# Keeping each 32-column block of a triangular inverse contiguous in SBUF

## The chip, the core and the metric

The kernel runs on one core of a Trainium2 chip. The metric is the device time of one execution in microseconds (us). The engines are TensorE (PE; its weight loads are shown as PEld), VectorE (DVE), ScalarE (ACT), GpSimd (POOL) and SyncE (SP, which issues the DMAs); each works through its own instructions in order. SBUF is the memory on the core with 128 partitions, PSUM the smaller one that TensorE writes.

## The reference, cut to what matters

Three stages follow each other: a linear recurrence over 768 steps for 32 heads of size 40, a channel mix, and an attention with four gated heads. The change touches the first alone:

```python
for t in range(S):                      # S = 768, state is (B, H, 40, 40)
    y[:, :, t] = np.einsum('bhd,bhde->bhe', rt, state)
    Sa = np.einsum('bhde,bhe->bhd', state, at)
    state = state * wt[:, :, None, :] - np.einsum('bhd,bhe->bhde', Sa, bt) \
            + np.einsum('bhd,bhe->bhde', vt, kt)
```

## The kernel before

The recurrence is done in 12 chunks of 64 steps. A chunk of half of the heads (16, as 8 pairs in the two halves of the partitions) is a unit `u`; there are 24 units, two to a chunk, and four units make a group `g`. Inside a chunk, the steps depend on each other through a unit lower triangular matrix of 64x64 per head, which has to be inverted. It is cut into two 32x32 diagonal blocks (inverted) and the 32x32 block below them (`m21`, used as it is).

- `front(u)` prepares a unit: scans for the decays on DVE (L152, L164), products (L172, L173), transposes on PE (L179, L189), and the matrices of the chunk as matmuls into PSUM (`pg`, L200). ACT evicts `pg`: the two diagonal blocks into `LX[g]` (L207, eight instructions a unit), the block `m21` (L210, four) and `ga` (L213).
- `lanes(g)` inverts all 128 x 2 diagonal blocks of a group at once on DVE. A 32x32 transpose (L226) brings `LX[g]` into `L`, so that each partition holds one block row by row. Thirty steps `s` follow, each a product (L231) and a sum (L233) over `(31 - s) x s` elements; memsets set the diagonal to 1 and what lies above it to 0 (L235, L239). A second transpose (L242) writes the inverses to `tf`.
- `core(u)` is the serial part. For each half `i` of 32 rows it multiplies by the inverse: 16 matmuls with 32x32 blocks of `tf` as weights (L276; each shows as two weight loads and two matmuls, so 32 of each a half). Between the halves come 16 matmuls with `m21` as weights (L270), which have the same sizes. ACT evicts `pw` at L256, L272, L279 and L283.
- `outs(u)` makes the outputs (L307 to L340).

`LX`, `L` and `tf` are 128 x 32 x 32 floats. In `L` a partition holds one block as `(t, s)`. In `LX` and in `tf` the two free axes are the column `t` within a block and the number `x` of the block in the group.

The strings `FIRST`, `STEADY` and `TAIL` say in which order the pieces of the sequences are written for a chunk; the instructions of PE keep that written order, those of the other engines are set by a scheduler at build time. After the recurrence, at about 480 us, the channel mix and the attention follow; they share no tile with the change.

Of the kernel before, what the change touches and what calls it, by code (L numbers as in the profile page):

```python
# [15 lines left out]
AF = mybir.ActivationFunctionType  # L16
# [12 lines left out]
PP = 8  # L29
WLEN = PP * C + 2 + PP  # L30
LDW = 3 * PP * C + WLEN
HP = PP // 2
# [13 lines left out]
def recurrence(ctx, tc, ld, vin, rv, ident, xs, keep, wpool, mix):  # L46

    nc = tc.nc
# [59 lines left out]
    BK, GA, PC, LX, M21, TF = {}, {}, {}, {}, {}, {}  # L108
# [33 lines left out]
    def front(u):  # L142

        g, uu = divmod(u, GU)
        c, bp = divmod(u, NBP)
        t = slot(u)
        f3 = t[:, :3 * PP * C].rearrange("p (k q t) -> p k q t", k=3, t=C)
        w = t[:, 3 * PP * C:3 * PP * C + PP * C + 2]
        last = t[:, 3 * PP * C + PP * C + 2:]

        P = keep.tile([128, PP, C], F32, tag="P", bufs=2, name=f"P{u}")
        nc.vector.tensor_tensor_scan(P.rearrange("p s t -> p (s t)"), w[:, :PP * C], onehot, 0.0, op0=OP.mult,  # L152
                                     op1=OP.add)
        pc = PC[u] = const.tile([128, PP, 2], F32, tag="pc", bufs=AHEAD + 3, name=f"pc{u}")
        nc.vector.tensor_scalar(pc[:, :, 0], P[:, :, C - 1], -1.0, None, op0=OP.mult)
        nc.vector.tensor_tensor(pc[:, :, 1], pc[:, :, 0], last, op=OP.mult)
        rc = fpool.tile([128, PP, 2], F32, tag="rc", bufs=2, name=f"rc{u}")
        nc.vector.reciprocal(rc, pc)
        E = etile
        early = u < GU  # L160
        ih = invhot.rearrange("p (s t) -> p s t", t=C)
        nc.vector.tensor_copy(ih[:, :, C - 2:], rc)
        er = E.rearrange("p s t -> p (s t)")[:, ::-1]
        nc.vector.tensor_tensor_scan(er, w[:, PP * C + 1:1:-1], invhot[:, ::-1], 0.0, op0=OP.mult, op1=OP.add)  # L164
        nc.vector.tensor_copy(E[:, :, C - 1], rc[:, :, 1])
        bkt = keep.tile([128, PP, 2, C], F32, tag="bkt", bufs=2, name=f"bkt{u}")
        if u >= GU:
            blank(u)
        ga = GA[u]
        for r in range(2):  # L170
            q = slice(64 * r, 64 * r + 64)
            nc.vector.tensor_tensor(ga[q, r], f3[q, 2], P[q], op=OP.mult)  # L172
        latest["dve"] = nc.vector.tensor_tensor(bkt.rearrange("p q k t -> p k q t"), f3[:, :2],  # L173
                                                E[:, None].to_broadcast([128, 2, PP, C]), op=OP.mult)
        yield

        pt = ps.tile([128, 4, 2, 64], F32, tag="f", bufs=3, name=f"pt{u}")
        for p in range(4):
            nc.tensor.transpose(pt[:, p].rearrange("p r e -> p (r e)"),  # L179
                                P[:, 2 * p:2 * p + 2].rearrange("p b t -> p (b t)"), ident)  # L180
        nc.scalar.activation(xs[bp][:, c].rearrange("p (a b d) -> p a b d", a=4, b=2), pt[:, :, :, :D], AF.Copy,
                             scale=-1.0)
        yield

        BK[u] = wpool.tile([128, PP, 2, D], F32, tag="bk", bufs=AHEAD + 4, name=f"bk{u}")
        for h in range(2):
            pb = ps.tile([128, HP, 128], F32, tag="f", bufs=3, name=f"pb{u}_{h}")
            for p in range(HP):
                nc.tensor.transpose(pb[:, p], bkt[:, h * HP + p].rearrange("p k t -> p (k t)"), ident)  # L189
            latest["act"] = nc.scalar.activation(BK[u][:, h * HP:h * HP + HP],  # L190
                                                 pb.rearrange("p q (r e) -> p q r e", r=2)[:, :, :, :D], AF.Copy)
            yield

        m21 = M21[u] = const.tile([128, PP, 32], F32, tag="m21", bufs=AHEAD + 1, name=f"m21{u}")
        if uu == 0:
            LX[g] = fpool.tile([128, 32, 32], F32, tag="lx", name=f"lx{g}")
        for h in range(2):
            pg = ps.tile([128, HP, 2, C], F32, tag="o" if early else "f", bufs=3, name=f"pg{u}_{h}")
            for p in range(HP):
                nc.tensor.matmul(pg[:, p], bkt[:, h * HP + p].rearrange("p k t -> p (k t)"),  # L200
                                 ga[:, :, h * HP + p], start=True, stop=True)
            hs = slice(h * HP, h * HP + HP)
            for r in range(2):
                for i in range(2):
                    q = slice(64 * r + 32 * i, 64 * r + 32 * i + 32)
                    x0 = uu * PP + h * HP
                    nc.scalar.activation(LX[g][q, :, x0:x0 + HP].rearrange("p t q -> p q t"),  # L207
                                         pg[q, :, r, 32 * i:32 * i + 32], AF.Copy)
                q = slice(64 * r, 64 * r + 32)
                nc.scalar.activation(m21[q, hs], pg[q, :, r, 32:], AF.Copy)  # L210
                z = slice(64 - 64 * r, 128 - 64 * r)
                if not early:
                    nc.scalar.activation(ga[z, r, hs], pg[z, :, r], AF.Copy)  # L213
                    if h:
                        latest["pool"] = nc.gpsimd.affine_select(ga[z, r], ga[z, r], [[0, PP], [1, C]], OP.is_gt, 0.0,  # L215
                                                                 base=0, channel_multiplier=-1)
                else:
                    nc.vector.tensor_tensor(ga[z, r, hs], pg[z, :, r],
                                            mask[z, None, :].to_broadcast([64, HP, C]), op=OP.mult)
            yield  # L220

    def lanes(g):

        L = fpool.tile([128, 32, 32], F32, tag="lt", name=f"lt{g}")
        Lf = L.rearrange("p t s -> p (t s)")
        nc.vector.transpose(Lf, LX[g].rearrange("p t x -> p (t x)"))  # L226
        for s in range(1, 31):
            tmp = fpool.tile([128, 16 * 16], F32, tag="tmp", bufs=1, name=f"tmp{g}_{s}")
            n = 31 - s
            tv = tmp[:, :n * s].rearrange("p (t c) -> p t c", c=s)  # L230
            latest["dve"] = nc.vector.tensor_tensor(tv, L[:, s + 1:, s:s + 1].to_broadcast([128, n, s]),  # L231
                                                    L[:, s:s + 1, :s].to_broadcast([128, n, s]), op=OP.mult)
            nc.vector.tensor_tensor(L[:, s + 1:, :s], L[:, s + 1:, :s], tv, op=OP.add)  # L233
            yield
        nc.vector.memset(Lf[:, ::33], 1.0)  # L235
        b = 16
        while b:

            nc.vector.memset(bass.AP(L.tensor, L.offset + b, [list(L.ap[0]), [66 * b, 16 // b], [32, b], [1, b]]), 0.0)  # L239
            b //= 2  # L240
        tf = TF[g] = tfs[g % 2]
        nc.vector.transpose(tf.rearrange("p t x -> p (t x)"), Lf)  # L242
        yield

    def core(u):

        g, uu = divmod(u, GU)
        c, bp = divmod(u, NBP)
        ga, bk, tf, U, T = GA[u], BK[u], TF[g], uv[u % 4], xu[bp]
        pw = ps.tile([128, PP, D], F32, tag=f"c{bp}", bufs=1, name=f"pw{u}")  # L250
# [4 lines left out]
        w0 = const.tile([128, PP, D], F32, tag="w0", bufs=2, name=f"w0{u}")  # L255
# [4 lines left out]
        for r in range(2):  # L260
            q = slice(64 * r, 64 * r + 64)
            nc.vector.tensor_copy(T[q, :, r, :D], U[q, :, r])

        for i in range(2):
            qs = [slice(64 * r + 32 * i, 64 * r + 32 * i + 32) for r in range(2)]
            if i:
                for p in range(PP):
                    for r in range(2):
                        q0 = slice(64 * r, 64 * r + 32)
                        nc.tensor.matmul(pw[qs[r], p], M21[u][q0, p], U[q0, p, r], start=False, stop=True,  # L270
                                         skip_group_check=True)
                nc.scalar.activation(w0, pw, AF.Copy)  # L272
                yield
            for p in range(PP):
                for r in range(2):
                    nc.tensor.matmul(pw[qs[r], p], tf[qs[r], :, uu * PP + p], w0[qs[r], p], start=p == 0,  # L276
                                     stop=True, skip_group_check=True)
            for r in range(2):
                nc.scalar.activation(U[qs[r], :, r], pw[qs[r]], AF.Copy)  # L279
            if i:  # L280
                for r in range(2):
                    q, z = slice(64 * r, 64 * r + 64), slice(64 - 64 * r, 128 - 64 * r)
                    nc.scalar.activation(T[z, :, r, :D], pw[q], AF.Copy)  # L283
            yield
        if c < NC - 1:
# [6 lines left out]
            for r in range(2):  # L292
                q = slice(64 * r, 64 * r + D)
# [646 lines left out]
```

## Time and profile before

| | us |
|---|---|
| median of 3 runs | 964.96 (963.48 to 965.97) |
| span of the profiled execution, from its first to its last instruction | 957.7 |
| median less that span | 7.3 |
| recurrence within the span, roughly | 0 to 480 |
| VectorE, TensorE, ScalarE busy over the span | 670.5, 810.1, 547.3 |

The time of the profiled execution itself is not listed; its span and the 7.3 us that lie around it stand for it. In the rows further down, "busy" is the time in which an engine works on instructions, "idle before" what it waited in front of them, with the instruction that ended the wait. The chain is the sequence of work that ended last, followed back from the end: time saved on it can shorten the execution, time saved beside it can not, until the chain moves. [...]

### The profile page before, as it was taken

What the parts mean: (1) busy time and instruction counts of PE and PEld (TensorE: products, weight loads), DVE (VectorE), ACT (ScalarE), POOL (GpSimd) and SP (SyncE); (2) the same over time, 40 slices, a digit from 0 to 9 for tenths busy, and PEclk for the clock granted to TensorE, in tenths of its full rate; (3) what the DMA queues carried; (4) which work ended last, traced back from release to release, by engine and by line L of the source; (5) the groups of instructions that cost most, each with busy time, mean ns of one, the idle gap of its engine ahead of it and who ended that gap; (6) DMA issues with size and microseconds to landing.
All of it is one profiled execution on the core that took longest, in us unless ns stands there. A gap on an engine that the chain in (4) does not pass through costs nothing.

```text
span 957.7 us, 22274 instructions
## 1 busy us (share of the span) xinstructions
PE 810.1 (85%) x8812; PEld 692.4 (72%) x8812; DVE 670.5 (70%) x1642; ACT 547.3 (57%) x1392; POOL 256.1 (27%) x332
## 2 busy tenths in 40 slices
PE   1554388884986889878899999999998999999997
PEld 1543377784886778857778788887887888788885
DVE  7988989789989976978766232322325886878874
ACT  2786187777677776646533242222315866767773
POOL 7001032123113210134434132201202633444330
PEclk9777579998898999979899999999999999999999
DMA  6423033423323221433321001000000001010001
GB/s 132 116 69 97 1 72 71 99 70 84 77 66 84 66 59 40 110 94 100 101 84 30 1 22 31 1 1 1 1 1 1 1 1 42 2 42 1 29 15 42
DMA packets 57895, 46.80 MB, mean 49 GB/s; under 512 B 45248, under 2 KB 48960, under 8 KB 55872
## 3 DMA queue, kind: packets, MB, share of 16 engines
q1 hardware_dynamic: 57792, 45.38, 18.8%
q8 instruction: 70, 1.15, 0.5%
q14 instruction: 33, 0.27, 0.1%
HBM read 41.44 MB, written 3.93 MB: 47 GB/s over the span
## 4 chain that ended last, share of the span: by engine, by line
PE 61%; DVE 16%; ACT 15%; DMA 5%; issue 3%; POOL 1%; SPq 0%; DVEq 0%; ACTq 0%; POOLq 0%
PE pn L322 5%; PE po L835 4%; PE pw L276 4%; ACT lx L207 3%; PE tp L822 3%; PE ph L635 3%; PE pa L654 3%; PE ph L632 3%; PE pa L653 3%; PE pa L652 3%; PE ph L633 3%; PE ph L631 3%; DMA ldt<-in_ld 3%; PE ps L782 2%; ACT ga L213 2%
## 5 line engine op out<-in xcount | busy, mean ns | idle before, releaser
L639 DVE SCALAR_TENSOR_TENSOR hl<-ph,hh 128x512 fp32r<-128x512 f32 x60 | 41.2, 690 | 122.4 <-ACT hh L638 121.1
L805 POOL TENSOR_TENSOR P<-P,sm 128x128 f32<-128x128 f32 (+2 forms) x92 | 82.9, 931 | 126.6 <-DVE sm L795 114.3
L215 POOL TENSOR_SCALAR_AFFINE_SELECT ga<-ga 64x512 f32<-64x512 f32 x40 | 36.6, 915 | 269.1 <-ACT ga L213 260.0
L276 PE MATMUL pw<-w,tf 32*32 32x40 f32 x1536 | 52.7, 235 | 53.5 <-DVE tf L242 45.3
L638 ACT ACTIVATE hh<-ph 128x512 fp32r<-128x512 f32 x60 | 35.2, 595 | 107.1 <-PE pa L654 95.9
L276 PEld LDWEIGHTS pw<-w,tf 32*32 32x32 f32 x1536 | 48.4, 150 | 58.6 <-issue 36.8
L207 ACT ACTIVATE lx<-pg 32x128 f32<-32x128 f32 x192 | 73.2, 381 | 14.9 <-PE pg L200 6.7
L786 ACT ACTIVATE P<-ps,mx 128x640 f32<-128x640 f32 (+4 forms) x96 | 60.5, 634 | 22.6 <-DVE mx L784 14.6
L189 PE MATMUL pb<-ident,bkt 128*128 128x128 f32 x192 | 33.8, 312 | 44.5 <-ACT ga L213 21.4
L279 ACT ACTIVATE uv<-pw 32x320 f32<-32x320 f32 x96 | 41.1, 428 | 52.7 <-PE pw L276 51.1
L233 DVE TENSOR_TENSOR lt<-lt,tmp 128x30 f32<-128x30 f32 (+9 forms) x180 | 63.5, 353 | 3.7
L784 DVE CUSTOM_DVE_ANT_0 ps<-ps,neg 128x640 f32<-128x640 f32 (+4 forms) x96 | 59.1, 640 | 7.5 <-PE ps L782 6.4
L231 DVE TENSOR_TENSOR tmp<-lt 128x30 f32<-128x30 f32 (+9 forms) x180 | 60.9, 338 | 3.2
L322 PE MATMUL pn<-rbd,uvt 128*128 128x128 f32 x384 | 60.8, 321 | 1.3 <-ACT uvt L311 1.3
L200 PE MATMUL pg<-ga,bkt 128*128 128x128 f32 x384 | 55.8, 304 | 5.7 <-ACT ga L213 5.5
L189 PEld LDWEIGHTS pb<-ident,bkt 128*128 128x128 f32 x192 | 23.4, 156 | 51.5 <-ACT ga L213 26.3
L322 PEld LDWEIGHTS pn<-rbd,uvt 128*128 128x128 f32 x384 | 57.1, 234 | 4.6 <-ACT uvt L311 2.2
L200 PEld LDWEIGHTS pg<-ga,bkt 128*128 128x128 f32 x384 | 52.7, 218 | 6.8 <-ACT ga L213 6.0
L822 PE MATMUL tp<-ident,P 128*128 128x128 f32 x336 | 52.0, 276 | 1.8 <-ACT pt L826 1.0
L668 POOL TENSOR_TENSOR t<-t,ul 128x512 f32<-128x512 f32 x12 | 15.3, 1295 | 119.9 <-DVE t L667 119.8
L654 PE MATMUL pa<-hh,w 128*128 128x512 f32 x120 | 47.0, 392 | 0.0
L632 PE MATMUL ph<-ul,w 128*128 128x512 f32 x120 | 46.8, 390 | 0.2 <-DVE ul L621 0.2
(220 smaller groups left out, 2364.2 us busy)
## 6 DMA issues: line engine op xcount, KB each, us to landing
ldt<-in_ld SPq DMA_DIRECT2D x44, 321.6 KB
uv<-in_vin SPq DMA_DIRECT2D x48, 80.0 KB
rbd<-in_rin SPq DMA_DIRECT2D x48, 80.0 KB
rpt<-in_rin SPq DMA_DIRECT2D x48, 80.0 KB
uvt<-in_rin SPq DMA_DIRECT2D x48, 80.0 KB
out<-o SPq DMA_DIRECT2D x24, 160.0 KB
ldt<-in_w SPq DMA_DIRECT2D x4, 512.0 KB
ldt<-in_w SPq DMA_DIRECT2D x5, 320.0 KB
```

The costliest lines, as they stand in the source:

```text
L200: nc.tensor.matmul(pg[:, p], bkt[:, h * HP + p].rearrange("p k t -> p (k t)"), ga[:, :, h * HP + p], start=True, stop=True)
L207: nc.scalar.activation(LX[g][q, :, x0:x0 + HP].rearrange("p t q -> p q t"), pg[q, :, r, 32 * i:32 * i + 32], AF.Copy)
L231: latest["dve"] = nc.vector.tensor_tensor(tv, L[:, s + 1:, s:s + 1].to_broadcast([128, n, s]), L[:, s:s + 1, :s].to_broadcast([128, n, s]) ...
L233: nc.vector.tensor_tensor(L[:, s + 1:, :s], L[:, s + 1:, :s], tv, op=OP.add)
L276: nc.tensor.matmul(pw[qs[r], p], tf[qs[r], :, uu * PP + p], w0[qs[r], p], start=p == 0, stop=True, skip_group_check=True)
L322: nc.tensor.matmul(pn[:, p], ut[:, h * HP + p].rearrange("p r t -> p (r t)"), rbd[u % 2][:, :, h * HP + p], start=True, stop=True)
L632: nc.tensor.matmul(ph, w[:, 0, f], ul[:, ft], start=False, stop=False)
L654: nc.tensor.matmul(pa[ft], w[:, 2 * DM - FT[2][0] + o:2 * DM - FT[2][0] + o + m], hh, start=False, stop=last)
L784: nc.vector.tensor_tensor_reduce(ps[:, :k], ps[:, :k], neg[:, S - k:], -1.0, 3e38, op0=OP.add, op1=OP.min, accum_out=mx[:, i:i + 1])
L786: nc.scalar.activation(P[blk][:, off[i] - off[i0]:off[i + 1] - off[i0]], ps[:, :k], AF.Exp, bias=mx[:, i:i + 1], scale=-1.0, accum_out=sm[ ...
L805: nc.gpsimd.tensor_tensor(p, p, sm[:, i:i + 1].to_broadcast([128, w]), op=OP.mult)
L822: nc.tensor.transpose(pt[:, j - j0], P[:, c:c + 128], ident)
```

## The change

`LX` and `tf` exchange their two free axes: from `(t, x)` to `(x, t)`, so that the 32 columns of a block lie next to each other. Four instructions see it.

- The ACT evictions into `LX` (L207) wrote single elements 32 floats (128 bytes) apart; they now write 128 elements in a row.
- The weight loads of `tf` (L276) read single elements 128 bytes apart; they now read 32 in a row.
- The first DVE transpose (L226) read in a row; it now reads single elements 128 bytes apart.
- The second DVE transpose (L242) wrote in a row; it now writes single elements 128 bytes apart.

```diff
-                    nc.scalar.activation(LX[g][q, :, x0:x0 + HP].rearrange("p t q -> p q t"),
-                                         pg[q, :, r, 32 * i:32 * i + 32], AF.Copy)
+                    nc.scalar.activation(LX[g][q, x0:x0 + HP], pg[q, :, r, 32 * i:32 * i + 32], AF.Copy)
...
-        nc.vector.transpose(Lf, LX[g].rearrange("p t x -> p (t x)"))
+        nc.vector.transpose(L, LX[g].rearrange("p x t -> p t x"))
...
-        nc.vector.transpose(tf.rearrange("p t x -> p (t x)"), Lf)
+        nc.vector.transpose(tf.rearrange("p x t -> p t x"), L)
...
-                    nc.tensor.matmul(pw[qs[r], p], tf[qs[r], :, uu * PP + p], w0[qs[r], p], start=p == 0,
+                    nc.tensor.matmul(pw[qs[r], p], tf[qs[r], uu * PP + p], w0[qs[r], p], start=p == 0,
```

No instruction is added, removed or moved: PE, DVE, ACT, POOL and SP each have the same instructions in the same order before and after. The changed program has one line less, so that what was L210 is L209 in it, and so on down; only L207 and the lines ahead of it keep their numbers.

On DVE, here is the end of `lanes` for the second group, with the transpose of the next group behind it. Before (the names are tiles with a number):

```order
L233 TENSOR_TENSOR lt_810<-lt_810,tmp_30_1150 128x30
L158 RECIPROCAL rc_1871<-pc_1868 128x16
L242 STREAM_TRANSPOSE tf_119<-lt_810 128x1024
L162 COPY invhot<-rc_1871 128x8x2
L172 TENSOR_TENSOR ga_1877<-ldt_84,P_1866 64x512 x2
L226 STREAM_TRANSPOSE lt_1650<-lx_1030 128x1024
```

The same place in the changed program:

```order
L232 TENSOR_TENSOR lt_810<-lt_810,tmp_30_1150 128x30
L158 RECIPROCAL rc_1871<-pc_1868 128x16
L241 STREAM_TRANSPOSE tf_119<-lt_810 128x32x32
L162 COPY invhot<-rc_1871 128x8x2
L172 TENSOR_TENSOR ga_1877<-ldt_84,P_1866 64x512 x2
L225 STREAM_TRANSPOSE lt_1650<-lx_1030 128x1024
```

Nothing moved. The transpose into `tf` now has an output pattern of 32 x 32 single elements; that of the other is on its input, which the row does not show.

## Rows read from the trace of the kernel before

**Rows 1.** Busy time of the engines in two stretches (instructions in brackets), granted clock.

```profile
112.00:340.00 228.00, 185.20 (x3545) 170.52 (x3546) 205.62 (x483) 172.47 (x483) 52.11 (x84) 0.89 0.32 73
363.00:416.00 53.00, 43.04 (x978) 38.85 (x974) 45.73 (x127) 33.64 (x89) 5.19 (x13) 0.91 0.30 77
```

**Rows 2.** Chain that ended last, shares by line in 0:112, 112:367 and 367:480 us.

```profile
by line: DMA ldt<-in_ld 23.1%; DVE P L152 11.0%; DVE ga L172 9.1%; DVE bkt L173 8.3%; DVE lt L233 7.7%; DVE tmp L231 6.9%; DVE E L164 6.3%; issue 4.6%; DVE pc L155 4.0%; DVE ga L218 3.3%; DVE invhot L162 2.0%; PE pb L189 1.7%; DVE rc L158 1
...
by line: ACT lx L207 12.8%; PE pn L322 12.4%; PE pw L276 9.2%; ACT ga L213 7.1%; PE pg L200 5.5%; ACT m L210 5.0%; issue 4.8%; ACT xu L283 4.7%; PE pb L189 4.6%; PE pw L270 4.4%; ACT uv L279 4.4%; ACT uvt L311 3.8%; PE pt L179 3.0%; ACT sbd
...
by line: PE pn L322 15.8%; PE pw L276 11.9%; DMA ldt<-in_w 11.0%; PE py L336 6.1%; PE py L332 4.3%; issue 4.1%; PE pv L307 3.8%; PE pw L270 3.5%; PE pw L253 3.0%; DVE ldt L455 3.0%; PE px L290 3.0%; DMA ldt<-in_v 2.7%; DMA room<-in_w 2.5%; 
```

**Rows 3.** Groups of instructions by line and shape: busy us, mean ns of one.

```profile
L207 ACT ACTIVATE lx<-pg 32x128 f32<-32x128 f32 x192 | 73.2, 381 | 14.9 <-PE pg L200 6.7 <-DVE ga L218 4.3 <-DVE lt L226 2.8
...
L213 ACT ACTIVATE ga<-pg 64x256 f32<-64x256 f32 x80 | 30.2, 378 | 1.0
...
L210 ACT ACTIVATE m<-pg 32x128 f32<-32x128 f32 x96 | 25.6, 267 | 1.2
...
L226 DVE STREAM_TRANSPOSE lt<-lx 128x1024 f32<-128x1024 f32 x6 | 7.4, 1241 | 4.7 <-ACT lx L207 4.3
L242 DVE STREAM_TRANSPOSE tf<-lt 128x1024 f32<-128x1024 f32 x6 | 7.4, 1236 | 0.1
```

**Rows 4.** Stretches with L276 alone, then L270 alone: PE, PEld busy, clock.

```profile
209.90:212.10 2.20, 2.03 (x64) 1.91 (x64) 1.00 0.30 84
111.90:113.40 1.50, 1.28 (x32) 1.15 (x32) 0.50 0.00 0
...
207.20:208.70 1.50, 1.34 (x64) 1.22 (x64) 1.00 0.25 57
120.20:121.60 1.40, 1.27 (x32) 1.10 (x32) 0.50 0.04 12
```

**Rows 5.** DVE groups by shape: L233 of step 1 (113.5 us), of step 30 (110.4 us).

```profile
L233 DVE TENSOR_TENSOR lt<-lt,tmp 128x30 f32<-128x30 f32 x1 | 0.2, 213 | 0.0
...
L233 DVE TENSOR_TENSOR lt<-lt,tmp 128x30 f32<-128x30 f32 x1 | 0.2, 191 | 0.0
```

**Rows 6.** Memsets of 32 elements by line, all of the span.

```profile
L239 DVE MEMSET lt<- 128x32 f32 x6 | 0.5, 85 | 0.0
L235 DVE MEMSET lt<- 128x32 f32 x6 | 0.5, 85 | 0.0
```

**Rows 7.** What DVE waited for in 112:367: us in total, times, longest.

```profile
DVE bkt L173 <- PE pg L200: 8.0, 6, 2.0
DVE P L152 <- PE pt L179: 6.6, 4, 2.5
DVE lt L226 <- ACT lx L207: 4.3, 1, 4.3
DVE nt L324 <- PE pn L322: 2.8, 2, 2.6
DVE nt L324 <- PE py L336: 2.2, 1, 2.2
DVE x L340 <- PE py L336: 0.8, 2, 0.5
```

**Rows 8.** The chain in order of time: transposes on it (start us, us).

```profile
58.66 1.14 DVE lt L226
...
110.60 1.26 DVE tf L242
...
237.88 1.26 DVE tf L242
...
303.84 1.26 DVE tf L242
```

**Rows 9.** The same chain: first and last of nine pieces of L276 at full clock.

```profile
139.95 2.00 PE pw L276 x64
...
346.40 1.07 PE pw L276 x32
```

## The prediction

> **What bounds the kernel now.** The change touches the recurrence only, so I first cut its 480 us by what the chain that ended last runs over, line by line [rows 2]. Up to 112 us it is VectorE work and DMA loads. From 112 to 367 us it changes hands between ScalarE and TensorE: the evictions into `LX` (L207) are its largest line with 12.8%, the matmuls with `tf` (L276) have 9.2%. From 367 to 480 us no `front` is left, so L207 is gone, and L276 has 11.9%. Both lines that the change should speed up therefore lie largely on the chain.
>
> The second thing to see is how close VectorE is behind. From 112 to 340 us it is busy for 205.6 of 228 us, 90% [rows 1]. Its waits show what it could give up if the others got faster: 8.0 + 6.6 + 4.3 + 2.8 + 2.2 + 0.8 = 24.7 us between 112 and 367 us, all of them for TensorE or ScalarE [rows 7]. And where a group of inverses is just finished, the chain runs through VectorE: the transpose into `tf` stands on it at 110.6, 237.9 and 303.8 us, with matmuls of L276 waiting behind it, and one transpose out of `LX` at 58.7 us [rows 8]. So ScalarE and TensorE set the pace, with VectorE in second place by some 10%; and the change gives to the first two and may take from the third.
>
> **ScalarE, L207.** It has 192 instructions of 32x128 at a mean of 381 ns. L210 moves the same shape out of the same PSUM tile, but writes in a row, and takes 267 ns [rows 3]. Nothing else separates the two, so I price the new L207 at 267 ns: 114 ns less each, 21.9 us of ScalarE work in all. A check on the reason: L213 moves 256 elements a partition in 378 ns, so a contiguous element costs (378 - 267) / 128 = 0.87 ns, and the element of L207 costs 0.87 + 114 / 128 = 1.76 ns [rows 3]. What counts is the part on the chain: 12.8% of 255 us is 32.6 us, and 114 / 381 of it is **9.8 us** [rows 2, 3]. Before 112 us ScalarE is not what is waited for, and I count nothing there.
>
> **TensorE, L276.** At full clock, 64 matmuls with `tf` take 2.03 us; 64 with `m21`, of the same sizes and with weights in a row, take 1.34 us. At half clock 32 of either take 1.28 and 1.27 us [rows 4]. [...] From 367 to 480 us it is 11.9% of 113 us, or 13.4 us [rows 2]; the clock in most of it is 0.91 on average [rows 1], and groups behind a wait tend to get the half clock, so I take two thirds: 13.4 x 2/3 x 0.34 = **3.0 us**.
>
> **What VectorE leaves of that.** The 9.8 + 3.6 = 13.4 us between 112 and 367 us are to come out of VectorE's waits of 24.7 us. That is enough in sum, but the waits come in lumps of up to 4.3 us [rows 7], and where there is none, an earlier ScalarE only waits for VectorE. I take off a sixth: 11.2 us.
>
> **VectorE, the two transposes.** There are six of each, 1.24 us apiece [rows 3], and each now has one side in single elements 128 bytes apart. No row shows a transpose of that kind, so I bound its cost. From below: a memset of 32 elements takes 85 ns in pairs (L239) and 85 ns as single elements 33 floats apart (L235) [rows 6]; by that the step is free. From above: a doubling of the whole instruction, as one element of ScalarE's doubled, is 1.24 us more. Between: in step 1 the sum at L233 reads and writes 30 single elements 128 bytes apart and takes 213 ns, in step 30 it has 30 in a row and takes 191 ns [rows 5]: 22 / 30 = 0.73 ns an element, or 0.75 us for 1024. I take the last, as it is the same engine and the same step, and as ScalarE's strided element with its 1.76 - 0.87 = 0.89 ns more is not far from it.
>
> [...]
>
> Which of the twelve lie on the path: two before 112 us [rows 8], where VectorE is the chain (1.5 us). Between 112 and 367 us there are eight; two stand on the chain and the two right behind them delay the next steps of VectorE, while the others run into VectorE's waits, so I count four (3.0 us). After that, L226 of the last group at about 363 us and L242 at about 415 us enclose the last 30 steps in a stretch where VectorE is busy for 45.7 of 53 us [rows 1]: both count (1.5 us). The four transposes that I take as hidden would cost up to 3.0 us more if the waits that cover them go; that is within the range below.
>
> **The sum.** Before 112 us: -1.5. Up to 367 us: 11.2 - 3.0 = 8.2. After: 3.0 - 1.5 = 1.5. Together 8.2 us saved. The profiled execution has a span of 957.7 us, which with the 7.3 us around it is the median of 964.96 us by construction; so the span becomes 949.5 and the time **956.8 us**.
>
> **The rivals.** A measurement of this kernel can tell about 0.3% from no change, that is 2.9 us: faster is below 962.1, slower above 967.9 us.
>
> 1. *Strides are free for VectorE* [rows 6]: the gross of 11.2 + 3.0 = 14.2 us stays, 950.8 us. Against it speak the 22 ns of rows 5.
> 2. *The transposes double* (1.24 us more): about nine are then on the path, 11.2 us, and 3.0 us are left: 962.0 us. ScalarE's doubled element speaks for it [rows 3], L233 against. [...]
> 3. *VectorE is the bound already.* Its waits go only where they are largest, in the chunk before 363 us: 16 evictions (1.8 us) and two groups of L276 (0.7 us). With 3.0 us at the end and eight transposes (6.0 us) that makes -0.5 us: 965.5 us. For it speaks the 90% [rows 1]; against it that 8.0 + 6.6 us of the waits are spread over ten places [rows 7]. It is also what happens if L207 does not come down to the duration of L210.
> 4. *The transposes triple*, the rival on the other side: 2.48 us more each, ten of them on the path, 24.8 us against 14.2: slower by 10.6 us, 975.6 us. It decides from (14.2 + 2.9) / 10 = 1.7 us more per transpose, a duration of about 2.95 us. For it speaks only that no row shows a transpose with a stepped side; against it every strided row of the trace, none of which costs more than double.
>
> **How the numbers follow.** I give the forecast (0.5 to 1.0 us more per transpose, 954 to 960 us) a chance of 0.45, rival 1 0.13, rival 2 0.16, rival 3 0.13, rival 4 0.13. Faster: 0.45 + 0.13 + 0.10 of rival 2 = 0.68. Same: 0.06 of rival 2 and 0.11 of rival 3 = 0.17. Slower: 0.13 + 0.02 = 0.15. The range leaves out rival 4 and the outer end of rival 1: 949.5 to 966 us.
>
> **What the changed profile would show.** L207 at 265 to 270 ns, and 64 matmuls of L276 (there L275) in about 1.35 us at full clock, unchanged at half clock. The transposes (there L225, L241) at about 2.0 us; 1.24 or 2.5 would be rivals 1 and 2, about 3.7 rival 4. VectorE's waits for TensorE and ScalarE between the first and the last `tf` should fall from 24.7 to some 10 us, and the first matmul of L275 should start about 1.5 us later than 112 us. If L207 and L275 have become faster and the waits are still there, the chain was not where I put it; if the waits are gone and the time has not changed, VectorE was the bound (rival 3).

## The result, and the profile after

The changed kernel takes 950.95 us at the median of four executions (948.57 to 952.18), the kernel before 964.22 us beside it; the ratio is 0.988, with an interval of 0.984 to 0.992. Two repetitions on other chips, told below, have 0.982 (0.980 to 0.985) and 0.987 (0.983 to 0.990). So the change gains 1.2 to 1.8%, 12 to 17 us in the three sets, where 8.2 us were predicted.

The groups that answer to [rows 3], with the new line numbers:

```profile
L207 ACT ACTIVATE lx<-pg 32x128 f32<-32x128 f32 x192 | 50.4, 263 | 20.0 <-PE pg L200 10.7 <-DVE ga L217 4.7 <-DVE lt L225 3.3
L212 ACT ACTIVATE ga<-pg 64x256 f32<-64x256 f32 x80 | 30.3, 379 | 1.0
L209 ACT ACTIVATE m<-pg 32x128 f32<-32x128 f32 x96 | 25.7, 268 | 1.2
L241 DVE STREAM_TRANSPOSE tf<-lt 128x1024 f32<-128x1024 f32 x6 | 11.6, 1927 | 0.1
L225 DVE STREAM_TRANSPOSE lt<-lx 128x1024 f32<-128x1024 f32 x6 | 11.6, 1926 | 2.7 <-ACT lx L207 2.4
```

The eviction into `LX` has come down to the duration of its neighbour, 263 against 268 ns, and ScalarE is busy 22.8 us less in that line. The transposes have gone from 1.24 to 1.93 us, alike for the one that reads single elements and the one that writes them: (1926 - 1241) / 1024 = 0.67 ns more an element. That is the size that L233 had shown with 0.73 ns [rows 5], and neither the free step of the memsets [rows 6] nor a doubling.

The matmuls with `tf`, as in [rows 4]: length of the stretch, PE busy, PEld busy, granted clock of TensorE as a share of full speed, DMA share, GB/s.

```profile
207.40:208.90 1.50, 1.34 (x64) 1.21 (x64) 1.00 0.64 143
112.10:113.50 1.40, 1.28 (x32) 1.14 (x32) 0.50 0.00 0
```

64 take 1.34 us at full clock instead of 2.03, and at half clock nothing has changed (32 take 1.28 us, as before). What VectorE waits for between the first `tf` and the last front, as in [rows 7]:

```profile
DVE bkt L173 <- PE pg L200: 3.8, 4, 1.7
DVE x L339 <- PE py L335: 3.0, 2, 1.7
DVE lt L225 <- ACT lx L207: 2.4, 1, 2.4
DVE P L152 <- PE pt L179: 1.4, 1, 1.4
DVE nt L323 <- PE py L335: 0.2, 1, 0.2
DVE nt L323 <- PE pn L321: 0.2, 1, 0.2
```

They have fallen from 24.7 to 11.0 us. The next rows are the three stages, cut at the first matmul with `tf`, at the first one of the ninth chunk (where no front is left) and at the channel mix. Each row has the length of the stage, the busy time of PE, PEld, DVE, ACT and POOL with the count, then clock, DMA share and GB/s; first the changed kernel:

```profile
0.00:112.17 112.17, 41.56 (x293) 37.77 (x294) 98.07 (x206) 53.73 (x158) 25.54 (x44) 0.78 0.35 89
112.17:355.78 243.61, 201.28 (x3996) 185.36 (x3997) 225.59 (x530) 178.86 (x545) 51.75 (x94) 0.87 0.33 74
355.78:471.77 115.99, 89.17 (x1904) 76.19 (x1904) 92.54 (x204) 64.66 (x161) 34.83 (x43) 0.90 0.34 91
```

then a second execution of the kernel before (span 963.4 us):

```profile
0.00:110.61 110.61, 42.70 (x292) 38.39 (x293) 97.13 (x206) 60.87 (x158) 25.89 (x44) 0.78 0.36 90
110.61:369.81 259.20, 211.17 (x3997) 194.95 (x3997) 223.42 (x533) 194.57 (x545) 57.16 (x94) 0.88 0.30 70
369.81:485.22 115.41, 96.93 (x1904) 83.82 (x1904) 92.64 (x201) 64.68 (x161) 34.80 (x43) 0.87 0.33 91
```

All of the gain of this pair is in the middle stage: 259.2 - 243.6 = 15.6 us. VectorE is now busy for 225.6 of its 243.6 us, 93% instead of 86%. The last stage has given nothing, although TensorE works 7.8 us less in it. Single traces scatter: two more of the changed kernel (told below) have 239.3 and 249.5 us in the middle stage and 116.2 and 114.8 us in the last, and the first trace of before had 255.2 and 112.8 us.

This second trace of before was needed because the first was not typical. In every execution listed, the time is 1.7 us more than the span (951.45 and 949.7 in the profiled one of the changed kernel; 965.08 and 963.4 in this one of before). The 7.3 us that the prediction put around the span were thus 1.7 us around it, and 5.6 us by which that execution was shorter than the median.

### The profile page after: what moved, and what is told of

Read it like the earlier page. It is cut to its first block, busy times and chain, and to the rows that moved or that the text cites. A ratio compares the mean times of both kernels' runs of the same rounds, so it can differ in the third digit from the quotient of the medians.

```text
span 949.7 us, 22274 instructions
## 1 busy us (share of the span) xinstructions
PE 797.7 (84%) x8812; PEld 680.4 (72%) x8812; DVE 674.9 (71%) x1642; ACT 525.3 (55%) x1392; POOL 251.2 (26%) x332
## 4 chain that ended last, share of the span: by engine, by line
PE 43%; DVE 7%; ACT 4%; DMA 3%; issue 1%; SPq 1%; POOL 1%; DVEq 0%; ACTq 0%; POOLq 0%
PE po L834 4%; PE tp L821 3%; PE ph L634 3%; PE pa L653 3%; PE ph L631 3%; PE pa L652 3%; PE pa L651 3%; PE ph L632 3%; PE ph L630 3%; PE ps L781 2%; PE ps L780 2%; DMA room<-in_w 1%; DMA ldt<-in_w 1%; PE pa L648 1%; PE pa L647 1%
## 5 line engine op out<-in xcount | busy, mean ns | idle before, releaser
L214 POOL TENSOR_SCALAR_AFFINE_SELECT ga<-ga 64x512 f32<-64x512 f32 x40 | 32.4, 810 | 254.2 <-ACT ga L212 245.7
L275 PE MATMUL pw<-w,tf 32*32 32x40 f32 x1536 | 40.8, 216 | 63.2 <-DVE tf L241 55.8
L275 PEld LDWEIGHTS pw<-w,tf 32*32 32x32 f32 x1536 | 36.4, 123 | 68.4 <-issue 48.0
L230 DVE TENSOR_TENSOR tmp<-lt 128x30 f32<-128x30 f32 (+9 forms) x180 | 63.2, 351 | 3.2
L200 PE MATMUL pg<-ga,bkt 128*128 128x128 f32 x384 | 60.0, 319 | 5.4 <-ACT ga L212 5.0
L232 DVE TENSOR_TENSOR lt<-lt,tmp 128x30 f32<-128x30 f32 (+9 forms) x180 | 61.5, 342 | 3.7
L207 ACT ACTIVATE lx<-pg 32x128 f32<-32x128 f32 x192 | 50.4, 263 | 20.0 <-PE pg L200 10.7
L200 PEld LDWEIGHTS pg<-ga,bkt 128*128 128x128 f32 x384 | 56.8, 233 | 6.4 <-ACT ga L212 5.6
L321 PE MATMUL pn<-rbd,uvt 128*128 128x128 f32 x384 | 58.2, 311 | 1.4 <-ACT uvt L310 1.4
L321 PEld LDWEIGHTS pn<-rbd,uvt 128*128 128x128 f32 x384 | 54.3, 224 | 4.6 <-ACT uvt L310 2.2
```

What stands on the lines that cost most here:

```text
L275: nc.tensor.matmul(pw[qs[r], p], tf[qs[r], uu * PP + p], w0[qs[r], p], start=p == 0, stop=True, skip_group_check=True)
L321: nc.tensor.matmul(pn[:, p], ut[:, h * HP + p].rearrange("p r t -> p (r t)"), rbd[u % 2][:, :, h * HP + p], start=True, stop=True)
```

## The experiments

Ratios are to the kernel before on the same chip, with intervals of 95%. As a scale: 0.990 is 9.6 us less.

**The two halves.** The LX half alone:

```diff
-                    nc.scalar.activation(LX[g][q, :, x0:x0 + HP].rearrange("p t q -> p q t"), ...
+                    nc.scalar.activation(LX[g][q, x0:x0 + HP], pg[q, :, r, 32 * i:32 * i + 32], AF.Copy)
-        nc.vector.transpose(Lf, LX[g].rearrange("p t x -> p (t x)"))
+        nc.vector.transpose(L, LX[g].rearrange("p x t -> p t x"))
```

> Only LX is turned: the evictions into it write in a row, the first transpose reads single elements 128 bytes apart; tf stays as before. The result of the computation is unchanged. Expected in either theory: L207 at 263 ns instead of 381, the first transpose at 1.93 us instead of 1.24, matmuls with tf still 2.03 us per 64. Theory A (ScalarE and TensorE set the pace and VectorE has waits to give up): five sixths of 9.8 us gained, three of six transposes on the path for 0.69 us each, so about 6 us less than before, 958. Theory B (VectorE is the bound): the six longer transposes cost 4 us and nothing is gained between 112 and 340 us; 0 to 2 us less or more than before, 962 to 966.

Measured: 950.66 us, ratio 0.985 (0.981 to 0.989). The transpose out of `LX` took 1.93 us, the one into `tf` 1.24 us. The tf half alone:

```diff
-        nc.vector.transpose(tf.rearrange("p t x -> p (t x)"), Lf)
+        nc.vector.transpose(tf.rearrange("p x t -> p t x"), L)
-                    nc.tensor.matmul(pw[qs[r], p], tf[qs[r], :, uu * PP + p], w0[qs[r], p], ...
+                    nc.tensor.matmul(pw[qs[r], p], tf[qs[r], uu * PP + p], w0[qs[r], p], ...
```

> Only tf is turned: the second transpose writes single elements 128 bytes apart, the weight loads of the matmuls with tf read in a row; LX stays as before. The result of the computation is unchanged. Expected in either theory: 64 matmuls with tf in 1.34 us at full clock and 2.5 us per 64 at half clock, second transpose at 1.93 us, L207 still 381 ns. Theory A: 3.0 + 3.0 us gained, five of six transposes on the path (3.5 us): about 2.5 us less than before, 962. Theory B: VectorE pays 4 us, and TensorE gains only at the end: 1 us more than before. If turning both is worth more than the sum of the halves, the halves share waits; if it is the sum, they are independent.

Measured: 965.91 us, ratio 1.001 (0.999 to 1.004). Next to these two, the LX half has all of the gain, more than twice what theory A gave it; the tf half gains nothing, which is nearer to theory B. Neither theory has both right.

**The price of the stepped transposes.** Both kernels leave one side of the exchange out, so that a duration can be had without its counterpart.

```diff
 # "no step": evictions and weight loads as in the change, transposes as before
+                    nc.scalar.activation(LX[g][q, x0:x0 + HP], ...
+                    nc.tensor.matmul(pw[qs[r], p], tf[qs[r], uu * PP + p], ...
 # "step only": the two transposes as in the change, the others as before
+        nc.vector.transpose(L, LX[g].rearrange("p x t -> p t x"))
+        nc.vector.transpose(tf.rearrange("p x t -> p t x"), L)
```

> As the changed kernel, but both transposes read and write in a row as before; the blocks are then permuted, so the inverses are not those of the reference, with the same instructions and sizes. It takes away the price of the stepped transposes alone, twelve times 0.69 us or 8.3 us of VectorE. Theory A: eight of the twelve lie on the path, so 5.5 us less than the changed kernel, 945. Theory B (VectorE is the bound after the change): 8 us less, 943. Theory C (the waits that the change left on VectorE hide them): at most 2 us less, 949.

Measured: 943.69 us, ratio 0.981 (0.977 to 0.985).

> The kernel before with the two transposes alone turned; evictions and weight loads stay as before, so the blocks are permuted and the inverses are not those of the reference, with the same instructions and sizes. It charges the price of the stepped transposes alone. Theory A: 8 of 12 on the path, 5.5 us more than before, 970. Theory B: all twelve, 8.3 us more, 972.5. Theory C: 2 us more at most, since VectorE's 24.7 us of waits take the rest, 966. If this cost is smaller than what the run without the steps gives back, the price of the steps depends on how fast the others are.

Measured: 966.53 us, ratio 1.002 (0.9995 to 1.0045). Alone, 8.3 us of VectorE work cost 2 us (0.5 us less to 4.3 us more by the interval), as theory C had it; that its waits take the rest is the reading that fits, and the interval leaves out the 5.5 and 8.3 us of theories A and B. Beside the faster engines the difference of the ratios (0.981 against 0.982 to 0.988 for the whole change) leaves 1 to 7 us, which does not separate the theories.

**Each saving without a price.**

```diff
 # evictions only
+                    nc.scalar.activation(LX[g][q, x0:x0 + HP], ...
 # weights only
+                    nc.tensor.matmul(pw[qs[r], p], tf[qs[r], uu * PP + p], ...
```

> The kernel before with the evictions into LX alone writing in a row; the first transpose reads in a row as well, so the blocks are permuted and the inverses are not those of the reference, with the same instructions and sizes. It measures the 118 ns that 192 ScalarE instructions lose, with no price on VectorE. The halves so far gave 13 us less (LX half, with its six stepped reads), 2 us more (tf half), 20 us less (both, no stepped transposes). Theory A (ScalarE sets the pace, TensorE's faster weight loads buy nothing by themselves): 16 to 18 us less than before, and weights alone 0 to 3 us less. Theory B (both buy something and each half's steps cost about the same): 14 us less here and 5 to 6 us less with the weights alone; the six stepped reads were then hidden.

Measured: 953.78 us, ratio 0.989 (0.987 to 0.992): 10.4 us less. That is less than either theory had.

> The kernel before with the weight loads of tf alone reading in a row; the second transpose writes in a row as well, so the blocks are permuted and the inverses are not those of the reference, with the same instructions and sizes. It measures 0.69 us per 64 matmuls at full clock with no price on VectorE. Prediction's step: 3.0 us between 112 and 367 us and 3.0 us after, 6 us less than before. Theory A: 0 to 3 us less. Theory B: 5 to 6 us less, which the six stepped writes of the tf half then used up (12 us of idle time of VectorE notwithstanding, since the transpose into tf is what TensorE waits for).

Measured: 964.45 us, ratio 1.0015 (0.999 to 1.004). The faster weight loads buy nothing by themselves, though the matmuls with `tf` went from 52.7 to 42.4 us in sum. Theory A has this one, at its edge. In this and the tf half, the mean granted clock over 12 executions each was 0.918 and 0.920, against 0.925 in 40 of the kernel before; and within one kernel a lower clock goes with a longer span (a correlation of -0.93 in the 12 with weights alone, -0.71 and -0.59 in two sets of before).

**Where TensorE's saving went.** To see it in a trace, both kernels were profiled a second time.

> The kernel before, unchanged, for a second trace: the one on which the prediction rests has a span of 957.7 us, while 40 timed executions have spans around 962. With faster weights alone, TensorE spent 10 us less on the matmuls with tf and 343 us instead of 328 on the other matmuls of the recurrence. Theory A (the faster weights themselves lower the granted clock): here the others take 328 to 332 us again, whatever the span. Theory B (the first trace was a lucky one): 335 us or more, near the 336 of the run with the stepped transposes alone.

> The run with faster weight loads alone (permuted blocks, inverses not those of the reference), for a second trace. Theory A: the other matmuls of the recurrence take 340 us or more again, and the granted clock between the first matmul with tf and the channel mix is again 0.81 to 0.87. Theory B: they take as long as in the second trace of the kernel before, within 3 us.

Measured: spans of 963.4 and 964.1 us. Groups of matmuls up to the channel mix, busy us and mean ns, and then the stretch from the first matmul with `tf` to the channel mix with all engines. The kernel before:

```profile
L200 PE MATMUL pg<-ga,bkt 128*128 128x128 f32 x384 | 58.1, 312 | 4.4 <-ACT ga L213 3.8 <-ACT bk L190 0.4 <-DVE pc L155 0.3
L276 PE MATMUL pw<-w,tf 32*32 32x40 f32 x1536 | 52.9, 236 | 52.6 <-DVE tf L242 44.2 <-ACT w L256 8.3
...
110.61:485.22 374.61, 308.10 (x5900) 278.76 (x5900) 316.06 (x733) 259.25 (x705) 91.95 (x137) 0.88 0.31 76
```

Weights only:

```profile
L200 PE MATMUL pg<-ga,bkt 128*128 128x128 f32 x384 | 63.6, 332 | 5.2 <-ACT ga L213 4.4 <-ACT bk L190 0.4 <-DVE pc L155 0.3
L276 PE MATMUL pw<-w,tf 32*32 32x40 f32 x1536 | 42.5, 221 | 55.5 <-DVE tf L242 45.6 <-ACT w L256 9.7
...
110.78:486.24 375.46, 300.64 (x5901) 271.30 (x5901) 315.89 (x733) 258.60 (x705) 91.09 (x137) 0.86 0.31 76
```

L276 saves 10.4 us, and L200, which nothing touched, takes 5.5 us more. Over the ten other matmul lines of the recurrence the sum is 334.2 us in the kernel before and 340.7 us with weights alone, 6.5 us more (328.1 us in the trace of the prediction, 343.0 and 343.5 us in the first traces of weights only and of the tf half). But a part of this lies ahead of the first matmul with `tf`, where no faster weight has been loaded yet: 45.3 against 47.6 us there, 23.3 against 25.3 us for L200. From that matmul on, L200 has 34.8 against 38.2 us, and the ten lines together have these sums:

| weight loads of `tf` | evictions into `LX` | the ten other lines, us, by trace |
|---|---|---|
| stepped | stepped | 285.3 and 288.8 (before), 287.0 (stepped transposes alone) |
| in a row | stepped | 299.9 and 293.0 (weights only), 295.6 (tf half) |
| stepped | in a row | 287.0 (evictions only), 287.1 and 287.3 (LX half) |
| in a row | in a row | 284.5, 284.0 and 290.9 (whole change), 285.8 (no step) |

So with weights alone, 4.2 of the 10.4 us saved in this pair were spent again in other matmuls, and some 9 us in the means of the first two rows of the table. Where the evictions are faster as well, the other matmuls take no longer than before (286.3 against 287.0 us in the mean). In this pair TensorE's idle time in the stretch grew by 8.3 us, and by 6.4 us of that TensorE waited longer for ScalarE. Three of these waits, in the same stretch (us in total, times, longest), first before, then with weights alone:

```profile
PE pb L189 <- ACT ga L213: 14.8, 8, 2.0
PE pw L276 <- ACT w L256: 8.3, 9, 1.2
PE pw L270 <- ACT uv L279: 0.2, 1, 0.2
```

```profile
PE pb L189 <- ACT ga L213: 17.7, 14, 2.0
PE pw L276 <- ACT w L256: 9.7, 9, 1.2
PE pw L270 <- ACT uv L279: 2.8, 3, 1.4
```

These three grew by 6.9 us; one for `sbd` at L315 fell by 0.6 us. Of the expectations, theory A had the weights right (340 us or more, and a clock of 0.86 between 0.81 and 0.87) and the kernel before wrong (334.2 us, not 328 to 332); theory B had neither (335 us or more; within 3 us of each other). The first trace was in part a lucky one, and the faster weights alone still lengthen the others.

**Blocks two and two.** The order in `LX` and `tf` is (pair of blocks, column, block of the pair), so that VectorE meets runs of two floats and the others step by two.

```diff
+                    xp = LX[g][q].rearrange("p a b -> p (a b)").rearrange("p (y t w) -> p y w t", y=16, w=2)
+                    nc.scalar.activation(xp[:, y0:y0 + HP // 2], pg[...].rearrange("p (y w) t -> p y w t", w=2), ...
+        nc.vector.transpose(L.rearrange("p t (y w) -> p t y w", w=2), LX[g]....rearrange("p (y t w) -> p t y w", ...))
```

> The changed kernel with blocks kept two and two: in LX and tf the order is (pair of blocks, column, block of the pair). The transposes then read and write runs of two adjacent floats, the evictions and the weight loads step by two floats (8 bytes). The result of the computation is unchanged. If a run of two is enough for each engine: transposes at 1.24 us, evictions at 263 ns, 64 matmuls with tf in 1.34 us, and the time of the run without stepped transposes, 7 us less than the changed kernel (944). If a step of 8 bytes costs ScalarE or TensorE as much as one of 128 bytes, evictions are at 381 ns and the time is that of the kernel before. If it costs half, about the changed kernel's time.

> The changed kernel again, beside the others on one chip, with more executions. If the halves add up (13 us less for LX, 2 us more for tf): 11 us less than before, 952.5. If turning both is worth more than its halves: 15 us less or more, 948.

Measured: 946.17 us, ratio 0.983 (0.979 to 0.988), for the pairs, and 946.63 us, 0.982 (0.980 to 0.985), for the whole change on the same chip. The groups of the kernel with pairs:

```profile
L209 ACT ACTIVATE lx<-pg 32x128 f32<-32x128 f32 x192 | 52.8, 275 | 18.2 <-PE pg L200 9.9 <-DVE ga L220 4.8 <-DVE lt L228 2.3
L278 PE MATMUL pw<-w,tf 32*32 32x40 f32 x1536 | 41.4, 218 | 58.2 <-DVE tf L244 50.0 <-ACT w L258 8.1
...
L228 DVE STREAM_TRANSPOSE lt<-lx 128x1024 f32<-128x1024 f32 x6 | 7.4, 1241 | 3.6 <-ACT lx L209 3.3
L244 DVE STREAM_TRANSPOSE tf<-lt 128x1024 f32<-128x1024 f32 x6 | 7.4, 1236 | 0.1
```

Every step is nearly free: 275 ns for the evictions, 1.24 us for the transposes, and the matmuls with `tf` as fast as in the change (218 ns in the mean, 41.4 us; 40.8 to 42.1 us in three traces of the change). Yet it is no faster than the change: a further sign that the 8.3 us of the transposes lie mostly beside the path.

The whole change stood here beside the single savings on the same chip, so that the parts can be set against the whole. Evictions alone have 953.78 us, weights alone gain nothing (964.45 us), and the whole change has 946.63 us: 7 us below the evictions alone (4 to 10 us by the scatter of five executions each), though it carries the stepped transposes that the evictions alone do not have. So on this chip the faster weights, worth nothing by themselves, count once the evictions are faster. The middle and the last stage of the evictions alone, then of the whole change:

```profile
110.77:360.10 249.33, 210.71 (x3996) 196.14 (x3997) 220.56 (x533) 179.07 (x545) 53.46 (x94) 0.85 0.32 73
360.10:471.87 111.77, 93.85 (x1904) 81.37 (x1904) 91.08 (x201) 64.50 (x161) 35.43 (x43) 0.89 0.35 94
```

```profile
112.34:351.65 239.31, 196.37 (x3996) 180.12 (x3996) 224.61 (x530) 178.88 (x545) 50.85 (x94) 0.90 0.33 76
351.65:467.82 116.17, 93.99 (x1905) 80.84 (x1905) 93.59 (x204) 64.46 (x161) 35.04 (x43) 0.85 0.33 90
```

In this pair the middle stage gains 10.0 us more and the last stage gives 4.4 us back.

**The halves once more, on one chip.**

> The LX half alone, on one chip with the whole change. So far it has a ratio of 0.985 to the kernel before, the whole change 0.988 and 0.982 on two other chips. Theory A (the tf half is worth something once ScalarE is faster): 3 us or more above the whole change. Theory B (the tf half is worth nothing in either case, its stepped writes and the lower clock take what its weight loads give): within 2 us of it.

> The whole change, on one chip with its LX half. Theory A: 3 us or more below the LX half, at 945 to 949. Theory B: within 2 us of the LX half.

Measured: 953.07 us, ratio 0.990 (0.987 to 0.993), for the LX half; 951.98 us, 0.987 (0.983 to 0.990), for the whole change. Their medians are 1.1 us apart, within theory B, their ratios 0.003 or 3 us, at the edge of theory A. By the scatter of six executions each, anything from 7 us less to 2 us more is possible, so these two runs cannot tell the theories apart, nor do they contradict the 7 us on the other chip.

## Why the prediction was right, and where not

The time of 950.95 us lies in the range of 949.5 to 966 us, at its lower end, and the sign is the one forecast. It lies outside the 954 to 960 us of the forecast itself, though, and on the 950.8 us of rival 1, for another reason than the rival's: the step on VectorE is not free, it is mostly hidden. The mechanism is right in its main part, ScalarE's evictions, and wrong in what TensorE and VectorE add to it. By its steps:

- **What bounds the kernel.** That ScalarE and TensorE set the pace with VectorE next is borne out for ScalarE: its evictions alone give 10.4 us. For TensorE by itself it is not: the line that had 9.2 and 11.9% of the chain could be made a fifth shorter with no effect on the time.
- **ScalarE, 9.8 us less a sixth.** The duration was right (263 ns for 267), and the part on the chain as well: 10.4 us measured (8.2 to 12.6 by the interval) against 9.8 us, or 8.2 us after the sixth was taken off. The runs show no need for the sixth, but do not rule it out.
- **TensorE, 3.6 + 3.0 us.** The saving per 64 matmuls was exact (2.03 to 1.34 us, none at half clock). What it is worth was wrong. No run shows the 3.6 us up to 367 us, which are 0.34, from (2.03 - 1.34) / 2.03 [rows 4], of the 10.6 us that nine pieces at full clock have on the chain [rows 9]; in place of both terms the runs showed nothing alone (964.45 us), and beside the faster evictions 7 us on one chip and 1 to 3 us on another. The step took the clock of every other matmul as fixed, and with weights alone it fell from 0.88 to 0.86 in the stretch; and it counted a piece on the chain as time saved, although TensorE reached the next wait for ScalarE sooner (6.4 us more of waiting for it in the pair of traces). That the faster weights by themselves lower the clock is shown by two kernels with them (0.918 and 0.920 in 24 executions) against one with the stepped transposes alone (0.924 in 12) and the kernel before (0.925 in 40). In the changed kernel the clock was 0.926, 0.931 and 0.924 in three sets of executions and is not lower; why it holds there is not shown.
- **The transposes, 0.75 us more each, eight on the path, 6.0 us.** The duration was near (0.69 us). The number on the path was the largest term mis-sized: charged alone they cost 2 us, not 6.0, as the waits of VectorE can take most of them. In the changed kernel itself the price is less certain: taking the steps away is worth 0 to 7 us there, by the pairs and by the run without steps. For the two in front of 112 us the traces do not decide: the first matmul with `tf` starts at 112.2, 112.3 and 110.6 us in the changed kernel, and at 112.0 and 110.6 us in that of before, where 1.5 us more were forecast.
- **The end, from 367 us.** 1.5 us were forecast and none came: the stage has 116.0, 116.2 and 114.8 us in the changed kernel, against 112.8 and 115.4 us before, so if anything it is longer. Two readings behind the 3.0 us of TensorE were weak. The clock of 0.91 [rows 1] covers 53 of the 113 us, less than half; over all of the stage it is 0.88 in that trace. (That groups behind a wait tend to get the half clock does hold there: the five stretches at half clock in the stage each begin in a wait of TensorE of 0.9 to 4.9 us or within 2 us behind it, and the 64 matmuls with `tf` behind the 4.9 us take 2.35 us at 0.50.) And the share of L276 on the chain, 11.9% in the trace of the prediction [rows 2], is 3.5% for the same matmuls in the first trace of the changed kernel, a fall far beyond the fifth by which they got shorter: the chain runs elsewhere there. What TensorE saves there goes in part into waiting for VectorE: for the last `tf` 8.9, 7.0 and 7.8 us in the three traces of the changed kernel, 4.9 and 6.0 us in the two of before. The rest differs by execution. In the first trace of the changed kernel VectorE waits longer for weights of the channel mix than in the second trace of before, as the rows below show (changed kernel, then before); in the second trace of the changed kernel TensorE's clock in the stage is 0.85, against 0.90 in the first.

```profile
DVE ldt L454 <- DMA ldt<-in_w: 9.5, 7, 2.9
DVE ldt L454 <- DMA ldt<-in_v: 3.1, 1, 3.1
```

```profile
DVE ldt L455 <- DMA ldt<-in_w: 6.7, 6, 2.6
...
DVE ldt L455 <- DMA ldt<-in_v: 2.5, 1, 2.5
```

- **The sum.** The prediction added its terms, each priced by itself. By the runs with single parts the sum would be 10.4 us for the evictions, nothing for the weights and 2 us less for the steps, or some 8 us, which is the 8.2 us forecast; the whole change has 12 to 17 us. So the single parts do not add up, and that the forecast agrees with their sum is luck: its 6.6 us for TensorE (none when alone) and its 6.0 us for the transposes (2 us when alone) nearly cancel, together with the sixth taken off. On the chip where the parts stood side by side the missing part is the one of TensorE, whose saving counts once the evictions are faster; its size, 1 to 7 us over two chips, stays open, and so does what the steps cost there. On a third chip the run without steps is 7 us below the LX half, which is both of these together.
- **The span.** That the span came out at 949.7 us for 949.5 forecast is chance: the trace of before that the sum started from was 5 us shorter than most executions.

Of the rivals, 1 (free strides) and 2 (doubling) fall by the 1.93 us, 4 (tripling) as well. Rival 3, VectorE as the bound, is not what the kernel before shows, as the evictions alone gain 10.4 us. The changed kernel has come closer to it, with VectorE busy for 93% of the middle stage; that it is the bound there is not shown, as the pairs, with 8.3 us less VectorE work, are no faster.

## What to carry to other kernels

Single elements 128 bytes apart had their own price on each engine here (118 of 381 ns for an eviction of 32x128, 0.69 of 2.03 us for 64 matmuls at full clock and nothing at half clock, 0.69 us on top of 1.24 for a transpose). So when a layout can serve only one side, read from comparable rows what each engine pays, and put the price on the engine that waits most. Then ask of each saving what its engine waits for next: TensorE's 10 us, saved alone, went into slower matmuls and into waits for ScalarE, and counted on one chip once ScalarE was faster too, while 8 us more on VectorE cost 2 us. So a saving that measures nothing alone should be measured again beside the others. And take the trace that a sum starts from against the listed executions: here it was one of the shortest.

## What the runs showed of the hardware that was not expected

- Faster weight loads by themselves lowered the granted clock of TensorE (0.918 and 0.920 in 24 executions, against 0.925 in 40 of the kernel before), and matmuls that nothing had touched took longer: L200 from 34.8 to 38.2 us over the 256 behind the first matmul with `tf`, with the mean clock of the stretch at 0.86 instead of 0.88. In the trace of the prediction 8 matmuls of L200 take 2.08 us at half clock (118.2 us), and 16 take 1.95 us at full clock (150.4 us). With the evictions faster too, the clock of the whole execution did not fall (0.924 to 0.931 against 0.925).
- A step of 8 bytes cost next to nothing where one of 128 bytes cost much: 275 ns against 381 for the eviction of 32x128 (263 in a row), and 41.4 us for the matmuls with `tf` against 52.7 to 53.5 us (40.8 to 42.1 in a row with the evictions faster too).
- A VectorE transpose paid the same 0.67 ns an element (1.24 to 1.93 us for 1024) whether its reading or its writing side is in single elements 128 bytes apart.
- Executions of one kernel differed by up to 12 us (958.59 to 970.63 us in 23 of the kernel before), the longer ones mostly at a lower granted clock (0.918 to 0.934, correlation -0.71).
